# Row gathers tied one by one to ScalarE steps instead of issued in rows, in a kernel of attention and eight routed experts

## The chip, the cores and the metric

The kernel runs on one core of one Trainium2 chip. Its engines are TensorE (PE: matrix products), ScalarE (ACT), VectorE (DVE), GpSimd (POOL: here it issues the indirect DMAs) and SyncE (SP: here it issues plain DMAs). Each takes its instructions in the order of the program and waits on semaphores that the others raise. The metric is device time in microseconds (us), less is better.

## The reference, cut to what matters

```python
qn = q / (norm(q, axis=1) + 1e-6); kn = k / (norm(k, axis=1) + 1e-6)     # 4 batches, 5056 x 256, f32
a = softmax(kn.T @ qn / tau);  x = (v @ a).reshape(20224, 256)
logits = x @ w_gate                                      # 8 experts, each takes 20224/8 = 2528 tokens
# tokens and experts are paired greedily by descending logit until every expert is full
for e in range(8):
    out[mask_e] = maximum(x[mask_e] @ w1[e], 0) @ w2[e]  # 256 -> 1024 -> 256
```

## The kernel before

The attention writes the rows of x to DRAM (`x_d`) in the first 305 us. After it the program goes through eight expert slots, p = 0 to 7; `route` finds out for slot p which expert it is and which tokens it has, in a stream of small DVE, ACT and PE instructions that a planner (`o`) strews between the expert work of the slot before. The order on each engine is fixed when the program is built.

A slot's 2528 tokens are cut into chunks of up to 512 rows (c = 0 to 4; slot 0 has six, the first and the last of them 256). A chunk goes through four steps. `load_x` puts its row gathers into the list `queue`, one for each 128 rows: an indirect DMA by POOL (L1483) from `x_d` into a tile `xg`, with a small memset of `spacer` (L1482) before it; behind the last gather of a chunk SP sends it out and back in blocks (L1468, L1473: tiles `xr`, `xq`). `turn` transposes it on DVE (L1528). `layer1` makes 8 units of 6 matmuls into a PSUM tile `ph`; ACT takes each unit's relu as `hH` (L1680), DVE the rest as `hL` (L1686). `layer2` makes a tile `py` of 24 matmuls for each 128 rows; ACT copies it to `y` (L1731) and POOL scatters it to `out` by an indirect DMA (L1734).

In slots 4 to 7 two chunks are taken together where `MIXED` says so: c = 3 with 4 in each, c = 1 with 2 in slots 6 and 7 too. Such a pair (`layers`) makes the first layer of both by 28 products of three matmuls (L1764) in the order of `STEPS`. Between the products ACT copies one PSUM tile onto another (`cAB`: `ph<-py`, `cBZ`: `ph<-ph`) or into the tile `p7` (L1770) and takes relus (`hi..`, L1790); DVE adds (`j..`, L1774) and makes the low parts (`lo..`, L1793). The next product into a tile waits for the copy.

A gather leaves `queue` at the calls of `gather()`: behind every second unit of `layer1` (every one in most of slot 0), behind each tile of `layer2`, all that are left in `turn_parts` and at the start of `layers`, and behind each product of a pair. None of these waits for the work at whose place it stands: it waits for its tile and its DMA semaphore only, so POOL may run them as soon as it is free. POOL also runs an `IOTA` (tile `G`) once for each route.

Of the kernel before, what the change touches and what calls it, by code (L numbers as in the profile page):

```python
# [14 lines left out]
AF = mybir.ActivationFunctionType  # L15
# [6 lines left out]
E, F = 8, 1024  # L22
# [72 lines left out]
PARTED = (4, 5, 6, 7)  # L95
MIXED = {4: (3,), 5: (3,), 6: (1, 3), 7: (1, 3)}
LOAD_AT = (1, 0)
STEPS = (
# [9 lines left out]
def attention_moe(ctx: ExitStack, tc: tile.TileContext, q, k, vt, tau, wg, w1t, w2t, tabs, out):  # L108
    nc = tc.nc
    V = nc.vector  # L110
    S = nc.scalar
    P = nc.gpsimd
# [7 lines left out]
    x_d = dram.tile([B * NCH * CH, C], F32, name="x_d")  # L120
# [485 lines left out]
    done = {}  # L606
# [719 lines left out]
    o = Order()  # L1326
# [26 lines left out]
    def n_in(col):  # L1353
        return 128 if col < NCOL - 1 else LASTC
# [99 lines left out]
    def load_x(p, c, paced=False):  # L1454
        idx = routed[p]["src"]
        if not chunks_seen:
            chunks_seen.append(ffx.tile([128, PAD_X], F32, name="pad_x", bufs=1))
        xg = ffx.tile([128, 4, C], F32, name="xg", bufs=2)
        xgs[p, c] = xg
        cols = cols_of(p, c)  # L1460
        by_v = (p, c) not in BY_PE
        xr = dram.tile([8, 128, 128], F32, name=f"xr{p}_{c}") if by_v else None

        def blocks():
            back = chunks.index((p, c)) - 2
            o.flush(turn_unit.get(chunks[back], 0))
            n = 2 * len(cols)
            nc.sync.dma_start(xr[0:n].rearrange("i p w -> p i w"), xg.rearrange("p i (k w) -> p (i k) w", k=2)[:, 0:n])  # L1468
            xq = ffx.tile([128, 4, 2, 4, 32], F32, name="xq", bufs=2)
            xgs[p, c] = xq  # L1470
            parts = xr[0:n].rearrange("i (g a) (j m) -> a (i g) j m", a=32, j=4)
            for j in range(4):
                nc.sync.dma_start(xq.rearrange("p i k g m -> p (i k g) m")[32 * j:32 * j + 32, 0:4 * n], parts[:, :, j])  # L1473

        def fetch(i, col, n):
            at = idx[:n, col:col + 1]
            if paced:
                at = ffx.tile([128, 1], I32, name="pace", bufs=4)[:n]
                S.activation(at, idx[:n, col:col + 1], AF.Copy)
            if by_v and n < 128:  # L1480
                P.memset(xg[n:128, i], 0.0)
            P.memset(spacer, 0.0)  # L1482
            P.indirect_dma_start(out=xg[:n, i, :], out_offset=None, in_=x_d,  # L1483
                                 in_offset=bass.IndirectOffsetOnAxis(ap=at, axis=0))
            if i == len(cols) - 1:
                if by_v:
                    blocks()
                landed[p, c] = o.pe + (MOVED_LAT if by_v else GATHER_LAT)
        for i, col in enumerate(cols):
            queue.append((p, c, lambda i=i, col=col, n=n_in(col): fetch(i, col, n)))  # L1490

    def gather():
        for _ in range(2 if queue and queue[0][1] == 0 else 1):
            if queue:
                queue.pop(0)[2]()

    queue = []
    landed = {}
# [22 lines left out]
    def turn_parts(p, c, xg, xH, xL, nt):  # L1521
        raw = ffx.tile([128, 2, 512], F32, name="xg", bufs=2)
        full = nt // 128

        def rotate(kb):
            rows = xg.rearrange("p i k g a -> p k i g a")[:, kb]
            turned_ = raw[:, kb].rearrange("p (i g n) -> p i g n", i=4, g=4)
            V.transpose(turned_[:, 0:full], rows[:, 0:full])  # L1528
            if nt % 128:
                V.transpose(turned_[:, full, 0:nt % 128 // 32], rows[:, full, 0:nt % 128 // 32])  # L1530
                V.memset(raw[:, kb, nt:512], 0.0)

        def mixed(dst, a, b, op):
            turned[0] = later_on(o.pe, 640, lambda: V.tensor_tensor(dst, a, b, op=op))

        def high(dst, src):
            def copy():
                S.activation(dst, src, AF.Copy)
                o.scalar(o.dve, 620)
            later_on(0, 0, copy)  # L1540

        def low(dst, src, h_):
            mixed(dst, src, h_.bitcast(F32), OP.subtract)
        for kb in range(2):
            turn_unit[p, c] = later_on(o.pe, 700, lambda kb=kb: rotate(kb))
        r1, r2 = raw[:, 0], raw[:, 1]
        high(xH[:, 1], r2)
        if c % 2:
            high(xH[:, 0], r1)
            low(xL[:, 1], r2, xH[:, 1])  # L1550
            low(xL[:, 0], r1, xH[:, 0])
            own["raw"] = r1, r2
            return
        a1, a2 = own["raw"]
        sH, sL = s_tiles()
        own["s"] = sH, sL
        low(xL[:, 1], r2, xH[:, 1])
        mixed(r2, r1, r2, OP.add)
        high(sH[:, 0], r2)
        mixed(r1, a1, r1, OP.subtract)  # L1560
        high(xH[:, 0], r1)
        mixed(a1, r2, a1, OP.subtract)
        high(sH[:, 1], a1)
        mixed(a2, a2, a1, OP.subtract)
        high(sH[:, 2], a2)
        low(xL[:, 0], r1, xH[:, 0])
        low(sL[:, 0], r2, sH[:, 0])
        low(sL[:, 1], a1, sH[:, 1])
        low(sL[:, 2], a2, sH[:, 2])
        while queue:  # L1570
            gather()
        at = chunks.index((p, c))
        for p_, c_ in chunks[at + 1:at + 3]:
            want(("idx", p_), lambda p_=p_, c_=c_: load_x(p_, c_))
# [84 lines left out]
    def layer1(p, c, inserts, every=1):  # L1659
# [9 lines left out]
        for fb in range(8):  # L1669
# [4 lines left out]
            for l, x_ in ((wH, xH), (wL, xH), (wH, xL)):  # L1674
                for kb in range(2):
# [1 line left out]
                    PE.matmul(ph[:, 0:nt], lhsT=l[:, w], rhs=x_[:, kb, 0:nt], start=(i == 0), stop=(i == 5))  # L1677
                    i += 1
                    o.tick(nt / 2.4 + 3)
            S.activation(hH[:, fb, 0:nt], ph[:, 0:nt], AF.Relu)  # L1680
            o.scalar(o.pe + 200, 600)

            lows[p, c] = unit[0]
# [3 lines left out]
                                       op0=OP.max, op1=OP.subtract)  # L1687
            o.post(o.pe + LAYER_LAT, 90 + nt, low, phs[-1])
            settle()
            if fb % every == (0 if p == 0 else every - 1):  # L1690
                gather()
        o.inner = False
        return hH, hL

# [13 lines left out]
    def layer2(p, c, h, inserts, behind=()):  # L1708
# [5 lines left out]
        for i, col in enumerate(cols_of(p, c)):  # L1714
# [23 lines left out]
            scat.append(sd)  # L1738
            settle()
            if not any(c + 1 in (f, f + 1) for f in MIXED.get(p, ())):  # L1740
                gather()

    def layers(p, c):
        o.flush(turned[0])
# [4 lines left out]
             "22": (bH[:, 1], bL[:, 1])}  # L1749
        for i, name in enumerate(("s1", "s2", "s4")):  # L1750
            x[name] = sH[:, i], sL[:, i]
        while queue:
            gather()
        h = [[ffx.tile([128, 8, 512], F32R, name=name) for name in ("hH", "hL")] for _ in range(2)]
        seeded = [(ph_tile(), len(phs) - 1) for _ in range(4)]
        fresh = [ps_2.tile([128, 512], F32, name="py") for _ in range(2)]
# [3 lines left out]
        def product(dst, a, b, g, first=False):  # L1760
            n = 0
            f = slice(g * 128, (g + 1) * 128)
            for i, l in ((0, 0), (0, 1), (1, 0)):
# [2 lines left out]
                n += 1  # L1766
                o.tick(227)

        def copy(dst, src):
            S.activation(dst, src, AF.Copy)  # L1770
            o.scalar(o.pe, 600)

        def joined(key, dst, src):
# [1 line left out]
            sums[key] = dst  # L1775
            o.dve += 690

        o.held = True
        for step in STEPS:
            op, g = step.split(".")  # L1780
            g = int(g)
            A, D = fresh[g % 2], fresh[1 - g % 2]
            Bk, Z = seeded[g % 2][0], seeded[2 + g % 2][0]
            if op[0] in "hl":
# [2 lines left out]
                t, f, src = place[op[2:]]  # L1787
                hH, hL = h[t]
                if op[0] == "h":
                    S.activation(hH[:, f], src, AF.Relu)  # L1790
                    o.scalar(o.pe, 600)
                else:
                    V.scalar_tensor_tensor(hL[:, f], src, 0.0, hH[:, f].bitcast(F32), op0=OP.max, op1=OP.subtract)  # L1793
                    o.dve += 690
# [12 lines left out]
            else:  # L1807
# [2 lines left out]
                 "P5": lambda: product(Z, "s1", "t1", g), "P4": lambda: product(Bk, "22", "t4", g),  # L1810
                 "P3": lambda: product(Z, "s4", "22", g)}[op]()
                settle()
                gather()
        o.held = False
        o.dve = max(o.dve, o.pe + PAIR_LAT)
        unit[0] += 1
# [219 lines left out]
```

## Time and profile before

| | us |
|---|---|
| time of the kernel, median of 3 runs (lowest, highest) | 1292.16 (1287.87, 1292.93) |
| the profiled execution's own time | 1292.82 |
| its span in the trace | 1291.0 |
| PE busy in it | 1241.5 (96%) |
| DVE, ACT, POOL busy | 945.2, 644.8, 404.6 |
| mean granted clock of TensorE, share of full | 0.993 |

The span is that of the instructions; the 1.8 us between it and the time lie around it. PE's idle time is the difference of span and busy time. Times in rows count from the span's start.

### The profile page before, as it was taken

Reading aid. Unit: us, or ns where it says so; the run is one execution under the profiler, and the core shown is the slowest. Engines: PE = TensorE matmul, PEld = TensorE weight load, DVE = VectorE, ACT = ScalarE, POOL = GpSimd, SP = SyncE. Lnnn points to the kernel's source line nnn. Section 1 sums busy time; section 2 is a strip of 40 time slices with the busy share of each in tenths; the row PEclk is TensorE's granted clock in tenths of the full one; section 3 lists DMA queues with packets and bytes.
Section 4 is the critical chain, followed back from the end, with each engine's and each line's share of the span. In section 5 each row is a group of like instructions: output and inputs, shape, how many; then the busy total and the mean of one; then the engine's idle time right before and its main releaser. Section 6 shows DMA issues by size and latency. Waiting matters only on the chain.

```text
span 1291.0 us, 23586 instructions
## 1 busy us (share of the span) xinstructions
PE 1241.5 (96%) x8710; PEld 1100.8 (85%) x8710; DVE 945.2 (73%) x2396; ACT 644.8 (50%) x1491; POOL 404.6 (31%) x700
## 2 busy tenths in 40 slices
PE   9999999999899999998999999999999999999998
PEld 7888877998788978887989879889889787978798
DVE  6687597888669678767777978787687776665652
ACT  6556652565324344433433745556564655554552
POOL 0000001001523445343444332634335444233422
PEclk9999999999999999999999999999999999999999
DMA  8999884344222154154432642442563443353500
GB/s 318 313 403 400 302 289 154 144 175 175 87 57 83 54 118 137 39 119 98 139 91 73 141 110 72 131 109 64 104 143 109 103 127 104 74 111 106 113 34 32
DMA packets 222515, 179.37 MB, mean 139 GB/s; under 512 B 152384, under 2 KB 193216, under 8 KB 217792
## 3 DMA queue, kind: packets, MB, share of 16 engines
q1 hardware_dynamic: 195328, 98.41, 28.1%
q0 software_dynamic: 17664, 58.22, 13.9%
q10 hardware_dynamic: 9408, 21.24, 4.2%
q8 instruction: 68, 1.11, 0.4%
q14 instruction: 47, 0.39, 0.1%
HBM read 118.06 MB, written 59.77 MB: 138 GB/s over the span
## 4 chain that ended last, share of the span: by engine, by line
PE 67%; issue 14%; POOL 8%; DMA 5%; DVE 3%; ACT 2%; another core or an unknown queue 0%; POOLq 0%; SPq 0%; ACTq 0%; DVEq 0%
PE py L1726 23%; PE ph L1677 22%; PE s L341 8%; PE px L289 8%; POOL out_dram L1734 4%; POOL xg L1483 3%; DMA x_d<-xs 2%; PE pc L853 2%; DMA ua<-in_q_dram 1%; PE px L467 1%; PE ph L1764 1%; DMA uc<-in_k_dram 1%; PE py L1764 1%; DVE hL L1686 1%; PE pi L1067 1%
## 5 line engine op out<-in xcount | busy, mean ns | idle before, releaser
L1726 PE MATMUL py<-uc,hH 128*128 128x256 f32 (+1 forms) x2560 | 339.4, 280 | 3.2 <-issue 3.2
L1726 PEld LDWEIGHTS py<-uc,hH 128*128 128x128 f32 (+1 forms) x2560 | 314.8, 187 | 7.0 <-issue 5.0
L1677 PE MATMUL ph<-xH,ua 128*128 128x512 f32 (+3 forms) x928 | 254.7, 392 | 3.7 <-issue 2.2
L1734 POOL DMA_INDIRECT out_dram<-y,idx x105 | 109.5, 1043 | 373.9 <-ACT y L1731 349.0
L1680 ACT ACTIVATE hH<-ph 128x512 fp32r<-128x512 f32 (+3 forms) x232 | 133.3, 579 | 157.3 <-PE ph L1677 138.3
L1677 PEld LDWEIGHTS ph<-xH,ua 128*128 128x128 f32 x928 | 168.2, 190 | 36.4 <-issue 4.2
L1686 DVE SCALAR_TENSOR_TENSOR hL<-ph,hH 128x512 fp32r<-128x512 f32 (+3 forms) x232 | 153.3, 663 | 52.2 <-ACT hH L1680 39.0
L1726 PE MATMUL py<-uc,hL 128*128 128x256 f32 (+1 forms) x1280 | 181.1, 279 | 1.7 <-issue 1.7
L1483 POOL DMA_INDIRECT xg<-x_d,src x156 | 155.0, 993 | 60.5 <-issue 56.5
L1726 PEld LDWEIGHTS py<-uc,hL 128*128 128x128 f32 (+1 forms) x1280 | 161.4, 187 | 2.2 <-issue 2.1
L1677 PE MATMUL ph<-xL,ua 128*128 128x512 f32 (+3 forms) x464 | 143.2, 388 | 0.0
L1731 ACT ACTIVATE y<-py 128x256 f32<-128x256 f32 (+1 forms) x105 | 40.2, 383 | 163.0 <-PE py L1726 129.0
L1677 PEld LDWEIGHTS ph<-xL,ua 128*128 128x128 f32 x464 | 86.4, 190 | 17.6 <-issue 1.2
L341 PE MATMUL s<-ua 128*128 128x256 f32 x320 | 74.0, 388 | 3.3 <-DMA ua<-in_q_dram 2.0
L341 PEld LDWEIGHTS s<-ua 128*128 128x128 f32 x320 | 60.9, 193 | 15.5 <-issue 6.0
L292 ACT ACTIVATE xs<-px 128x512 f32<-128x512 f32 (+2 forms) x98 | 49.6, 519 | 47.4 <-PE px L289 45.5
L341 PE MATMUL s<-uc 128*128 128x256 f32 x320 | 71.4, 380 | 0.3 <-DMA uc<-in_q_dram 0.3
L341 PEld LDWEIGHTS s<-uc 128*128 128x128 f32 x320 | 60.3, 190 | 9.4 <-issue 1.5
L289 PE MATMUL px<-aH,vh 128*128 128x256 f32 (+1 forms) x232 | 67.7, 294 | 0.5 <-ACT aH L257 0.5
L289 PE MATMUL px<-aH,vl 128*128 128x256 f32 (+1 forms) x232 | 65.8, 284 | 1.4 <-DVE vl L268 1.4
L1734 POOL DMA_INDIRECT out_dram<-c,idx x33 | 34.0, 1030 | 104.2 <-ACT c L1731 101.6
L289 PE MATMUL px<-aL,vh 128*128 128x256 f32 (+1 forms) x232 | 65.7, 284 | 0.0
(431 smaller groups left out, 2178.4 us busy)
## 6 DMA issues: line engine op xcount, KB each, us to landing
x_d<-xs ACTq DMA_DIRECT2D x39, 512.0 KB
xr<-xg SPq DMA_DIRECT2D x34, 512.0 KB
xq<-xr SPq DMA_DIRECT2D x136, 128.0 KB
vr<-in_vt_dram SPq DMA_DIRECT2D x14, 1024.0 KB
uc<-in_k_dram SPq DMA_DIRECT2D x18, 512.0 KB
uc<-in_q_dram SPq DMA_DIRECT2D x18, 512.0 KB
ua<-in_k_dram SPq DMA_DIRECT2D x17, 512.0 KB
ua<-in_q_dram SPq DMA_DIRECT2D x17, 512.0 KB
```

The costliest lines, as they stand in the source:

```text
L289: mm = PE.matmul(px[:, i * C:i * C + width], lhsT=l_, rhs=a_, start=(j == 0), stop=(j == len(terms) - 1))
L292: S.activation(xs[:, t % TH:t % TH + n, 0:width], px[:, 0:n * width].rearrange("p (t c) -> p t c", t=n), AF.Copy)
L341: newest[0] = PE.matmul(sb[:, ib * C:(ib + 1) * C], lhsT=kt[:, t, ib * 128:(ib + 1) * 128], rhs=qt[:, t, :], start=(first and t == 0 and i ...
L853: PE.matmul(D, lhsT=ge[:, g], rhs=oh[:, 0:Q, cs_], start=(g == 0), stop=(g == COLS // CG - 1))
L1483: P.indirect_dma_start(out=xg[:n, i, :], out_offset=None, in_=x_d, in_offset=bass.IndirectOffsetOnAxis(ap=at, axis=0))
L1677: PE.matmul(ph[:, 0:nt], lhsT=l[:, w], rhs=x_[:, kb, 0:nt], start=(i == 0), stop=(i == 5))
L1680: S.activation(hH[:, fb, 0:nt], ph[:, 0:nt], AF.Relu)
L1686: V.scalar_tensor_tensor(hL[:, fb, 0:nt], ph[:, 0:nt], 0.0, hH[:, fb, 0:nt].bitcast(F32), op0=OP.max, op1=OP.subtract)
L1726: PE.matmul(py[:n, 0:C], lhsT=l[:, fb, tk], rhs=w[:, d], start=(j == 0), stop=(j == 23))
L1731: S.activation(y[:n], py[:n, 0:C], AF.Copy)
L1734: sd = P.indirect_dma_start(out=out, out_offset=bass.IndirectOffsetOnAxis(ap=idx[:n, col:col + 1], axis=0), in_=y[:n], in_offset=None)
L1764: PE.matmul(dst, lhsT=w[b][l][:, f], rhs=x[a][i], start=(first and n == 0), stop=(n == 2), skip_group_check=True)
```

## The change

Each gather of a slot other than 0 now waits, by a semaphore, for one ScalarE instruction: `gather(after)` hands it to `fetch`. In `layer1` one gather stands behind the relu of every unit but the first (slot 0 has its places of before, with the wait). In a pair one stands behind the last ACT step at each of 8 (c = 1) or 10 (c = 3) entries of `GATHER_AT`. In `layer2` none is left between the tiles, except in a slot's last chunk where the next chunk to be gathered is at most two ahead (`rush`); slot 0 keeps its own. The loops that emptied `queue` in `turn_parts` and `layers` are gone. Besides, `o.held`, which keeps the planner's streams out of a pair, is now set in a pair c = 3 only if the next slot's tokens are known by then.

```diff
+GATHER_AT = {1: ("p7.0", "cAB.1", "cBZ.1", "hi12.0", "cAB.2", "p7.2", "hi11.2", "cAB.3"),
+             3: ("p7.0", "cAB.1", "cBZ.1", "hi12.0", "hi21.1", "hi11.2", "cBZ.3", "hi11.3",
+                 "hi12.3", "hi21.3")}
...
-        def fetch(i, col, n):
+        def fetch(i, col, n, after=None):
...
-            P.indirect_dma_start(out=xg[:n, i, :], out_offset=None, in_=x_d,
+            got = P.indirect_dma_start(out=xg[:n, i, :], out_offset=None, in_=x_d,
                                  in_offset=bass.IndirectOffsetOnAxis(ap=at, axis=0))
+            if after is not None:
+                tc.add_manual_dep(got.ins, after.ins.name, SPACED, reason="room between gathers")
...
-    def gather():
-        for _ in range(2 if queue and queue[0][1] == 0 else 1):
-            if queue:
-                queue.pop(0)[2]()
+    def gather(after=None):
+        if queue:
+            queue.pop(0)[2](after)
... turn_parts, and the same in layers:
-        while queue:
-            gather()
... layer1:
-            S.activation(hH[:, fb, 0:nt], ph[:, 0:nt], AF.Relu)
+            relu = S.activation(hH[:, fb, 0:nt], ph[:, 0:nt], AF.Relu)
-            if fb % every == (0 if p == 0 else every - 1):
-                gather()
+            if fb % every == 0 if p == 0 else fb > 0:
+                gather(relu)
... layer2:
             if not any(c + 1 in (f, f + 1) for f in MIXED.get(p, ())):
-                gather()
+                rush = p and c == len(cuts[p]) - 1 and queue and chunks.index(queue[0][:2]) <= chunks.index((p, c)) + 2
+                for _ in range(int(bool(rush)) if p else 2 if queue and queue[0][1] == 0 else 1):
+                    gather()
... layers (last_act[0] is set by each copy and each hi step):
-        o.held = True
         for step in STEPS:
+            o.held = c < 3 or p == E - 1 or bool(done.get(("idx", p + 1)))
...
                 settle()
-                gather()
+            if step in GATHER_AT[c]:
+                gather(last_act[0])
```

On POOL, at the start of the pair c = 3 of slot 6, behind the last scatter of the chunk before, the rows before are

```order
L1734 DMA out_dram<-y,idx 20224x256 [waits DMASW6_49,Activation_49]
L1482 MEMSET spacer 1x1 [waits Pool_49]
L1483 DMA xg<-x_d,src 128x256 [waits DMAHW6_49,DMASW7_49,DVE_49]
L1482 MEMSET spacer 1x1 [waits Pool_49]
L1483 DMA xg<-x_d,src 128x256 [waits DMASW0_49]
L1482 MEMSET spacer 1x1 [waits Pool_49]
L1483 DMA xg<-x_d,src 128x256 [waits DMASW1_49]
```

and those of the changed kernel, in which the lines have moved by three or four, are

```order
L1738 DMA out_dram<-y,idx 20224x256 [waits DMASW6_49,Activation_49]
L1485 MEMSET spacer 1x1 [waits Pool_49]
L1486 DMA xg<-x_d,src 128x256 [waits DMASW7_49,DMAHW6_49,DVE_49,Activation_49]
L1485 MEMSET spacer 1x1 [waits Pool_49]
L1486 DMA xg<-x_d,src 128x256 [waits DMASW0_49,Activation_49]
L1485 MEMSET spacer 1x1 [waits Pool_49]
L1486 DMA xg<-x_d,src 128x256 [waits DMASW1_49,Activation_49]
```

POOL's order is the same here; what moved is the time at which each gather may start, by the added wait for ACT.

On POOL, in a slot without pairs, between two tiles of `layer2` of one chunk and `layer1` of the next, the rows before are

```order
L1734 DMA out_dram<-y,idx 20224x256 [waits DMASW1_49,Activation_49]
L1733 MEMSET spacer 1x1 [waits Pool_49]
L1734 DMA out_dram<-p_9618,idx 20224x256 [waits DMASW2_49,Activation_49]
L1482 MEMSET spacer 1x1 [waits Pool_49]
L1483 DMA xg<-x_d,src 128x256 [waits DMAHW6_49,DMASW3_49,DVE_49]
L1482 MEMSET spacer 1x1 [waits Pool_49]
L1483 DMA xg<-x_d,src 128x256 [waits DMASW4_49]
L1733 MEMSET spacer 1x1 [waits Pool_49]
L1734 DMA out_dram<-y,idx 20224x256 [waits DMASW5_49,Activation_49]
```

and those of the changed kernel are

```order
L1738 DMA out_dram<-p_9594,idx 20224x256 [waits DMASW2_49,Activation_49]
L1737 MEMSET spacer 1x1 [waits Pool_49]
L1738 DMA out_dram<-y,idx 20224x256 [waits DMASW3_49,Activation_49]
L1737 MEMSET spacer 1x1 [waits Pool_49]
L1738 DMA out_dram<-y,idx 20224x256 [waits DMASW4_49,Activation_49]
L1485 MEMSET spacer 1x1 [waits Pool_49]
L1486 DMA xg<-x_d,src 128x256 [waits DMASW5_49,DMAHW6_49,DVE_49,Activation_49]
L1485 MEMSET spacer 1x1 [waits Pool_49]
L1486 DMA xg<-x_d,src 128x256 [waits DMASW6_49,Activation_49]
```

The gathers have moved from between the scatters (L1738) to behind them, each behind a relu.

On ACT, at the start of the pair of slot 5, the rows before, in which `junk` and `ext` belong to the route of slot 6, are

```order
L1129 ACTIVATE junk,sgn<-pi,rhalf 128x160 [waits Activation_49] x2
L1131 ACTIVATE ext<-pi 128x6
L1731 ACTIVATE y<-py 128x256 [waits DMASW4_49,PE_49]
L1770 ACTIVATE ph<-py 128x512 [waits PE_49]
L1770 ACTIVATE p_13033<-py 128x512 [waits DMASW1_49,PE_49]
```

and those of the changed kernel are

```order
L1735 ACTIVATE y<-py 128x256 [waits DMASW4_49,PE_49]
L1132 ACTIVATE junk,sgn<-pi,rhalf 128x160 [waits Activation_49]
L1776 ACTIVATE ph<-py 128x512 [waits PE_49]
L1132 ACTIVATE junk,sgn<-pi,rhalf 128x160 [waits Activation_49]
L1134 ACTIVATE ext<-pi 128x6
L1776 ACTIVATE p_12966<-py 128x512 [waits DMASW1_49,PE_49]
```

Two `junk` and the `ext`, ahead of the last copy to `y` before, stand behind it now, two of the three between the pair's first two copies; the 16 small DVE instructions that follow on them in the route stand inside the pair too.

## Rows read from the trace of the kernel before

**Rows 1.** The page, parts 1 and 2: the span, PE's busy time

```profile
span 1291.0 us, 23586 instructions
...
PE 1241.5 (96%) x8710; PEld 1100.8 (85%) x8710; DVE 945.2 (73%) x2396; ACT 644.8 (50%) x1491; POOL 404.6 (31%) x700
```

**Rows 2.** Engines' busy us by stretch, clock, DMA, GB/s: five layer bursts

```profile
333.20:353.00 19.80, 16.05 (x107) 12.07 (x106) 12.73 (x31) 6.47 (x11) 13.56 (x24) 1.00 0.33 96
...
sum 74.10, PE 61.32 PEld 48.60 DVE 43.48 ACT 27.45 POOL 52.46; mean PE 12.26 PEld 9.72 DVE 8.70 ACT 5.49 POOL 10.49
```

**Rows 3.** The same view: the bursts at the starts of five pairs

```profile
1128.60:1142.00 13.40, 10.83 (x47) 8.02 (x45) 6.03 (x9) 7.51 (x14) 9.31 (x18) 1.00 0.52 140
...
sum 66.10, PE 53.52 PEld 39.94 DVE 32.55 ACT 37.19 POOL 46.26; mean PE 10.70 PEld 7.99 DVE 6.51 ACT 7.44 POOL 9.25
```

**Rows 4.** The same view: six more bursts

```profile
437.50:456.00 18.50, 16.61 (x172) 16.06 (x170) 10.90 (x33) 4.55 (x10) 13.15 (x24) 1.00 0.28 87
822.20:839.20 17.00, 14.97 (x72) 11.53 (x70) 11.78 (x34) 8.72 (x20) 12.11 (x19) 1.00 0.65 153
...
707.20:718.80 11.60, 11.60 (x58) 9.11 (x57) 11.27 (x27) 8.30 (x25) 8.99 (x15) 1.00 0.52 149
...
sum 80.10, PE 72.25 PEld 62.84 DVE 55.96 ACT 35.38 POOL 58.98; mean PE 12.04 PEld 10.47 DVE 9.33 ACT 5.90 POOL 9.83
```

**Rows 5.** PE alone by stretch: all between these bursts

```profile
353.00:437.50 84.50, 83.59 (x717) 0.98 0.22 62
...
768.80:822.20 53.40, 53.40 (x371) 0.97 0.36 95
...
910.20:945.50 35.30, 35.30 (x245) 0.96 0.44 105
...
1142.00:1162.90 20.90, 20.90 (x133) 0.92 0.45 82
...
sum 685.10, PE 681.17; mean PE 48.65
```

**Rows 6.** PE alone by stretch: the first 7.3 us of each pair burst

```profile
1128.60:1135.90 7.30, 7.30 (x33) 1.00 0.30 90
...
sum 36.50, PE 36.50; mean PE 7.30
```

**Rows 7.** POOL's timeline, pair of slot 6: start, us, instruction [idle before, releaser]

```profile
1128.60 0.97 POOL L1734 DMA_INDIRECT out_dram<-y,idx  x1 [1.66 <-ACT y L1731]
...
1129.87 0.98 POOL L1483 DMA_INDIRECT xg<-x_d,src  x1 [0.22 <-issue]
...
1138.66 0.94 POOL L1483 DMA_INDIRECT xg<-x_d,src  x1 [0.23 <-issue]
```

**Rows 8.** ACT's timeline in the same burst

```profile
1141.33 0.58 ACT L1770 ACTIVATE ph<-py 128x512 f32<-128x512 f32 x1 [2.86 <-remote]
```

**Rows 9.** PE's timeline in the same burst

```profile
1141.96 1.18 PE L1764 MATMUL ph<-sH,ub 128*128 128x512 f32 x2 [2.45 <-ACT ph L1770]
```

**Rows 10.** PE's waits over the span: total us, times, longest

```profile
PE ph L1764 <- ACT ph L1770: 9.3, 5, 2.5
```

**Rows 11.** ACT's timeline in the last pair, the one without gathers

```profile
1255.30 0.58 ACT L1770 ACTIVATE ph<-py 128x512 f32<-128x512 f32 x1
```

**Rows 12.** ACT's timeline in a layer1 of slot 3

```profile
708.67 0.60 ACT L1680 ACTIVATE hH<-ph 128x512 fp32r<-128x512 f32 x1
...
710.05 0.60 ACT L1680 ACTIVATE hH<-ph 128x512 fp32r<-128x512 f32 x1 [0.41 <-issue]
```

**Rows 13.** DVE's timeline at the start of slot 5's pair

```profile
1010.98 2.80 DVE L1166 TENSOR_SCALAR at<-sgn 128x12 int32<-128x12 f32 x1 [1.19 <-ACT junk L1129]
...
1016.29 0.69 DVE L1793 SCALAR_TENSOR_TENSOR hL<-py,hH 128x512 fp32r<-128x512 f32 x1 [0.24 <-issue]
```

**Rows 14.** SP's queue in the pair c = 1 of slot 6

```profile
1102.68 2.65 SPq L1473 DMA_DIRECT2D xq<-xr  x4
```

**Rows 15.** DVE's timeline in the same pair

```profile
1112.55 0.57 DVE L1528 STREAM_TRANSPOSE xg<-xq 128x384 f32<-128x384 f32 x1
```

More of the change, by code (lines that the diff above doesn't have):

```diff
@@ L1482, in fetch @@
             P.memset(spacer, 0.0)
-            P.indirect_dma_start(out=xg[:n, i, :], out_offset=None, in_=x_d,
-                                 in_offset=bass.IndirectOffsetOnAxis(ap=at, axis=0))
+            got = P.indirect_dma_start(out=xg[:n, i, :], out_offset=None, in_=x_d,
+                                       in_offset=bass.IndirectOffsetOnAxis(ap=at, axis=0))
+            if after is not None:
+                tc.add_manual_dep(got.ins, after.ins.name, SPACED, reason="room between gathers")
             if i == len(cols) - 1:
@@ L1489, in load_x @@
         for i, col in enumerate(cols):
-            queue.append((p, c, lambda i=i, col=col, n=n_in(col): fetch(i, col, n)))
-    def gather():
-        for _ in range(2 if queue and queue[0][1] == 0 else 1):
-            if queue:
-                queue.pop(0)[2]()
+            queue.append((p, c, lambda after, i=i, col=col, n=n_in(col): fetch(i, col, n, after)))
+    SPACED = mybir.DependencyInfo(mybir.DependencyClass.Sync, mybir.DependencyReason.DATA)
+    def gather(after=None):
+        if queue:
+            queue.pop(0)[2](after)
     queue = []
@@ L1751, in layers @@
             x[name] = sH[:, i], sL[:, i]
-        while queue:
-            gather()
         h = [[ffx.tile([128, 8, 512], F32R, name=name) for name in ("hH", "hL")] for _ in range(2)]
@@ L1767, in product @@
                 o.tick(227)
+        last_act = [None]
         def copy(dst, src):
-            S.activation(dst, src, AF.Copy)
+            last_act[0] = S.activation(dst, src, AF.Copy)
             o.scalar(o.pe, 600)
@@ L1789, in layers @@
                 if op[0] == "h":
-                    S.activation(hH[:, f], src, AF.Relu)
+                    last_act[0] = S.activation(hH[:, f], src, AF.Relu)
                     o.scalar(o.pe, 600)
@@ L1812, in layers @@
                 settle()
-                gather()
+            if step in GATHER_AT[c]:
+                gather(last_act[0])
         o.held = False
```

## The prediction

> **What bounds the kernel now.** I read the page first: TensorE (PE) is busy for 1241.5 of 1291.0 us [rows 1]. PE sets the end, so the question is only in what stretches the other 49.5 us of idle time and the losses of its clock lie. I listed PE's gaps over half a microsecond, saw that most stand where GpSimd (POOL) issues many indirect DMAs in a row, and cut the time from 333 to 1265 us by that: the view of windows shows five bursts of gathers in `layer1` and `layer2` with 61.32 us of PE in 74.10, so 12.78 idle [rows 2], five at the starts of pairs with 53.52 in 66.10, so 12.58 idle [rows 3], six others with 72.25 in 80.10, so 7.85 idle [rows 4]; in all that lies between, PE is busy for 681.17 of 685.10 us, 3.93 idle [rows 5]. So 33.2 of 37.1 idle us stand in 220 us of bursts.
>
> One burst shows what the bursts do. After a scatter at 1128.60 eight gathers follow, from 1129.87 to 1138.66, one every (1138.66 - 1129.87) / 7 = 1.256 us [rows 7]. Near its end PE stands still for 2.45 us for a copy `ph<-py` of ScalarE (ACT), which itself stood idle for 2.86 us, released by something that the profile can't name ("remote"), until 1141.33 [rows 8, 9]. The copy's input was long written. In the pair without gathers the same copy runs with no wait [rows 11]. Now (1141.33 - 1128.60) / 9 = 1.414 us: if each of the nine DMAs takes 1.41 us of something behind POOL through which the hand-overs between engines pass too, while POOL issues one each 1.256, the lag grows by 0.16 us a DMA, and what is handed over late in a burst comes late. It fits that PE is never idle in the first 7.3 us of the five pair bursts, in which the scatter and some five gathers go out (36.50 busy of 36.50 [rows 6]), so that all 12.58 idle us stand in what is left of them; 9.3 of these are waits for that copy, up to 2.5 each [rows 10]. I call it the backlog. It is inferred, not seen. The other 3.3 us are waits for other steps of ACT and DVE in the same late parts.
>
> A burst also costs clock. Right behind some of them the granted clock is at its lower level for a while, 1.2 of 2.4 GHz, which shows as means below 1.00: 84.5 us at 0.98 lose 1.7 us, 53.4 at 0.97 lose 1.6, 35.3 at 0.96 lose 1.4, 20.9 at 0.92 lose 1.7 [rows 5]. The bursts ahead of them hold the idle time above; in the stretches themselves PE is busy nearly throughout, so that this is work at half speed, on top of the idle time.
>
> **The change, part by part.**
>
> *Gathers of the pairs.* The rows of the order say that they keep their places on POOL and get a wait for ACT; 8 stand behind ACT steps that lie over some 12 to 15 us of the pair, one per 1.5 us or more in the mean, where POOL issued one per 1.256. Behind POOL stands nothing that the pair needs: only later gathers, and the scatters of the next tiles. At 1.41 us a DMA the lag is then at most that of two or three neighbouring steps. I take the whole 12.6 us as gained [rows 3]. Bounds: nothing, if the waits have another cause, and 12.6.
>
> *Gathers of the layers.* They leave the places between `layer2`'s scatters and stand one behind each relu. Two relus stand 1.38 us apart [rows 12], as long as a DMA takes by the backlog, so that four gathers of a chunk in four units build no lag of their own. But scatters that are late from the tiles before, and an expert's end with its `rush`, still put three to five DMAs behind one another; by the new order I count about a third of the old length in such places. So two thirds of 12.78 are gained, 8.5 us; bounds 4.3 and 12.8 [rows 2]. Of the other bursts, that of slot 4's start (822 us, 17.00 - 14.97 = 2.03 idle) is shortened, half is taken, 1.0; the rest keep their order [rows 4].
>
> *Clock.* The lower level behind the two pair bursts goes (1.4 + 1.7 = 3.1 us); of the two behind layer bursts (1.7 + 1.6) two thirds, 2.2. Together 5.3 [rows 5].
>
> *The route inside slot 5's pair.* By the new `o.held` its tail (two `junk`, the `ext`, some 16 small DVE instructions) moves inside. There it meets the `IOTA` of POOL, which the new order puts there too. Before, that same piece took DVE from 1010.98 to the pair's first operation at 1016.29, 5.31 us, of which 2.80 in one instruction on 12 elements a partition, beside which the `IOTA` ran [rows 13]. ACT's part is short, but DVE's stands ahead of the pair's `j` and `lo` steps, for which PE waits. Bounds: nothing (the pair's DVE has idle time) and 4.8 us (all but half a microsecond). I take the middle, 2.4, lost.
>
> *Late data.* In a pair c = 1 the last gather goes out some 3.3 us later, and the pair is some 2.5 us shorter. SP sent the last blocks from 1102.68, done at 1105.33; their transpose ran at 1112.55 [rows 14, 15], 7.2 us after. That leaves 7.2 - 5.8 = 1.4 us for the transfer itself. It may be late by about one microsecond in each of two pairs: bounds 0 and 2, taken as nothing, since DVE is far less busy than PE there (32.55 against 53.52 [rows 3]).
>
> *Added waits themselves.* A semaphore more on POOL's DMA costs PE nothing as such; the ACT steps have no new instruction.
>
> Sum: 12.6 + 8.5 + 1.0 + 5.3 - 2.4 = 25.0 us. The profiled execution took 1292.82, so 1267.8, rounded to **1268**. That execution is 0.66 above the median, less than the three runs differ (1287.87 to 1292.93); I don't correct for it. About 0.5%, 6.5 us, can be told from no change here.
>
> **The rivals.**
>
> *The gain stands in the pairs only (18%).* In the layers the 1.38 us between relus is a shade below 1.41, and the scatters come on top: the backlog may stay as it is, only later. For it: in the burst at 437 us gathers alternate with scatters and PE still loses 1.89 us [rows 4]. Against it: in the burst at 707 us seven gathers, a scatter and a weight load leave PE without any idle time [rows 4], so a little room is enough. Time: 1292.8 - 12.6 - 3.1 + 2.4 = 1279.5.
>
> *The waits have another cause (10%).* The bursts stand at the starts of pairs and ends of chunks, where PE depends on ACT and DVE anyway, and where the route's chains run. A rule by which DMAs could not hold up engines would say so. Then nothing but the route's move is felt: 1292.8 to 1295. Against it stands above all the pair without gathers, in which the copy `ph<-py` doesn't wait [rows 11], and the "remote" release [rows 8]. The Trainium skill has such a rule ("SBUF — State Buffer", section Who interferes with whom): DMA never contends with a compute engine for that memory's ports, and only VectorE and GpSimd share a pair. By that rule the sum would hold nothing of the bursts. The trace doesn't agree as far as waits go: 33.2 of 37.1 idle us lie in bursts; the rule speaks of ports only, not of hand-overs.
>
> *Slower: the gather delays the ACT step's hand-over (5%).* Each gather now starts just as the ACT step ends on which PE's next product waits. If POOL's issue (0.97 us [rows 7]) holds up that hand-over each time, rather than only when a lag has grown, the 40 gathers of five pairs cost 40 x 0.97 = 38.8 us, and the time is 1267.8 + 38.8 = 1306.6. It is slower than before from 25.0 / 40 = 0.63 us each. Against it: before, the first five gathers of each pair burst go out beside copies and relus without any idle time of PE [rows 6].
>
> *As forecast: 67%.* That case's own range: with all of the layers (12.8), the whole of 822's 2.0, the whole clock (6.4) and a free route the gain is 33.8, so 1259; with a third of the layers (4.3) and of their clock (1.1), nothing at 822, a route of 4.8 and late data of 2.0 it is 12.6 + 4.3 + 4.2 - 4.8 - 2.0 = 14.3, so 1278.5.
>
> **How the numbers follow.** Faster by over 0.5%: forecast and first rival, 0.67 + 0.18 = 0.85. Within 0.5%: 0.10. Slower: 0.05. The range of 1258 to 1286 holds the forecast's own range and the first rival with its dear route (1279.5 + 2.4, and 4 us for a part of the pairs' gain that fails); it leaves out the second and the third, 0.15, and little else.
>
> **What would show it.** In the changed kernel's trace: POOL's gathers in pairs 1.3 us or more apart in nearly all places; no `ph<-py` of ACT released by "remote"; PE's wait for ACT's `ph` in pairs near nothing, from 9.3 us; the stretches behind the first and fourth pair at a clock of 1.00; layer bursts with about 4 us of idle PE in all. In slot 5's pair one wait of PE of 2 us or so for DVE. The prediction is wrong if PE still waits at the same steps though the gathers are apart (the second rival), if many short waits of PE follow the ACT steps named in the table (the third), or if the idle time of the layers only moves to later units (the first).

## The result and the profile after

The changed kernel takes 1257.92 us (median of 4 runs, 1255.64 to 1259.74) against 1292.12 of before in the same place: 0.9731 of it, 95% interval [0.9708, 0.9755], 34.2 us less. The prediction was 1268 with a range that began at 1258. The profiled execution took 1259.74, 33.1 us less than that of before, and the parts below are told against these two.

One thing has to be known for all that follows. The runs of this study were made in jobs, each with runs of the kernel before beside it, and the kernel before took 1290 to 1297 us in some of them (that of the result too) and 1240 us in others. Ratios are formed within one job.

The page of the changed kernel, to be read beside [rows 1]:

```profile
span 1258.0 us, 23692 instructions
...
PE 1230.8 (98%) x8710; PEld 1099.2 (87%) x8710; DVE 944.8 (75%) x2396; ACT 646.0 (51%) x1491; POOL 400.0 (32%) x700
```

PE is idle for 1258.0 - 1230.8 = 27.2 us, 22.3 less than before, and busy for 10.7 less. To place both I cut the new trace at the same matmuls at which the windows of before begin and end. The five pair bursts, beside [rows 3]:

```profile
993.55:1005.11 11.56, 9.97 (x44) 7.88 (x44) 10.71 (x31) 7.31 (x14) 5.34 (x10) 1.00 0.13 35
...
1102.09:1112.45 10.36, 10.36 (x47) 8.28 (x46) 5.94 (x9) 7.94 (x14) 5.25 (x10) 1.00 0.22 63
...
sum 52.93, PE 51.34 PEld 41.23 DVE 35.32 ACT 38.77 POOL 27.06; mean PE 10.27 PEld 8.24 DVE 7.06 ACT 7.75 POOL 5.41
```

66.10 us have become 52.93, so 13.2 are gone; the idle time left, 52.93 - 51.34 = 1.59 us, all stands in slot 5's pair. PE's busy time fell too, from 53.52 to 51.34, with the same 231 matmuls. The five layer bursts, beside [rows 2]:

```profile
334.55:351.17 16.62, 15.42 (x107) 12.07 (x106) 12.56 (x31) 6.47 (x11) 11.18 (x21) 1.00 0.27 80
...
sum 62.57, PE 59.40 PEld 48.93 DVE 44.17 ACT 29.54 POOL 37.36; mean PE 11.88 PEld 9.79 DVE 8.83 ACT 5.91 POOL 7.47
```

74.10 have become 62.57, 11.5 gone, 3.17 idle left. (In one of the five, from 574.23 us, the route's small matmuls lie elsewhere, so that 63 stand in it in place of 49; those of the layer are the same to one.) Of the others [rows 4] I show slot 4's start (17.00 before), slot 5's end (11.50 before) and slot 6's end (12.90 before):

```profile
807.79:821.78 13.99, 13.99 (x70) 11.81 (x69) 12.21 (x26) 9.50 (x26) 8.42 (x16) 1.00 0.24 74
1022.98:1032.21 9.23, 9.23 (x83) 8.93 (x83) 8.16 (x17) 3.72 (x13) 7.83 (x12) 1.00 0.73 213
1131.77:1145.17 13.40, 10.43 (x86) 10.09 (x86) 5.91 (x10) 3.69 (x9) 9.49 (x17) 0.93 0.53 172
...
sum 75.09, PE 70.44 PEld 62.92 DVE 55.92 ACT 37.28 POOL 51.20; mean PE 11.74 PEld 10.49 DVE 9.32 ACT 6.21 POOL 8.53
```

The first has lost all its idle time, 3.0 us of length, and the second 2.3 us; in the third gathers still stand in a row behind scatters, and it has not gained. The stretches behind bursts, PE alone, beside the four of [rows 5]; the last one is the stretch behind slot 6's end, 25.90 us long before:

```profile
351.17:434.12 82.95, 82.03 (x717) 1.00 0.24 70
755.92:807.79 51.87, 51.87 (x372) 1.00 0.41 107
890.54:924.55 34.01, 34.01 (x247) 1.00 0.55 139
1112.45:1131.77 19.32, 19.32 (x134) 1.00 0.76 151
1145.17:1171.89 26.72, 26.72 (x160) 0.91 0.24 55
```

Four of them are at the full clock now and shorter by 1.55, 1.53, 1.29 and 1.58 us, 5.95 in all; the last is 0.82 longer. In the pair of slot 6, the one shown before, POOL's gathers now start like this:

```profile
1103.78 0.99 POOL L1486 DMA_INDIRECT xg<-x_d,src  x1 [0.64 <-ACT p L1776]
...
1105.99 0.96 POOL L1486 DMA_INDIRECT xg<-x_d,src  x1 [1.13 <-ACT ph L1776]
...
1112.76 0.94 POOL L1486 DMA_INDIRECT xg<-x_d,src  x1 [1.63 <-ACT hH L1796]
```

They are 2.2 and 2.3 us apart (1112.76 is the fifth), each released by ACT, where they were 1.25. The copy `ph<-py` that stood idle for 2.86 us before [rows 8] has no wait:

```profile
1111.26 0.58 ACT L1776 ACTIVATE ph<-py 128x512 f32<-128x512 f32 x1
```

### The profile page after: what moved, and what is told of

Read it like the earlier page. It is cut to its first block, busy times and chain, and to the rows that moved or that the text cites. A ratio compares the mean times of both kernels' runs of the same rounds, so it can differ in the third digit from the quotient of the medians.

```text
span 1258.0 us, 23692 instructions
## 1 busy us (share of the span) xinstructions
PE 1230.8 (98%) x8710; PEld 1099.2 (87%) x8710; DVE 944.8 (75%) x2396; ACT 646.0 (51%) x1491; POOL 400.0 (32%) x700
## 3 DMA queue, kind: packets, MB, share of 16 engines
q1 hardware_dynamic: 195328, 98.41, 28.1%
## 4 chain that ended last, share of the span: by engine, by line
PE 69%; issue 11%; POOL 6%; DMA 6%; DVE 5%; ACT 2%; POOLq 0%; SPq 0%; ACTq 0%; DVEq 0%
PE py L1730 23%; PE ph L1681 23%; PE px L292 8%; PE s L344 8%; POOL out_dram L1738 3%; POOL xg L1486 3%; DMA x_d<-xs 2%; PE pc L856 2%; PE ph L1768 2%; DMA ua<-in_q_dram 1%; PE px L470 1%; PE py L1768 1%; DMA uc<-in_k_dram 1%; PE pi L1070 1%; DMA uc<-in_q_dram 1%
## 5 line engine op out<-in xcount | busy, mean ns | idle before, releaser
L1681 PE MATMUL ph<-xH,ua 128*128 128x512 f32 (+3 forms) x928 | 251.5, 388 | 1.0 <-DVE xL L1618 0.9
L1738 POOL DMA_INDIRECT out_dram<-y,idx x105 | 108.0, 1029 | 290.1 <-ACT y L1735 264.9
L1738 POOL DMA_INDIRECT out_dram<-c,idx x33 | 33.1, 1002 | 81.8 <-ACT c L1735 80.7
```

The costliest lines, as they stand in the source:

```text
L1738: sd = P.indirect_dma_start(out=out, out_offset=bass.IndirectOffsetOnAxis(ap=idx[:n, col:col + 1], axis=0), in_=y[:n], in_offset=None)
```

## Experiments

Runs of one job shared a chip and the runs of the kernel before.

| job | run | us | before | ratio, 95% |
|---|---|---|---|---|
| 1 | e1 pairs only | 1239.95 | 1239.93 | 1.000 [0.999, 1.001] |
| 1 | e2 layers only, streams held | 1266.58 | | 1.0218 [1.020, 1.024] |
| 1 | e3 new order, no wait | 1244.20 | | 1.0038 [1.003, 1.005] |
| 1 | e4 before, three memsets | 1242.11 | | 1.0021 [1.001, 1.003] |
| 2 | e5 the change again | 1262.08 | 1296.41 | 0.9755 [0.972, 0.979] |
| 2 | e6 before, no memset | 1293.66 | | 0.9967 [0.994, 1.000] |
| 2 | e7 the change, streams held | 1279.09 | | 0.9884 [0.985, 0.992] |
| 3 | e8 as e1 | 1239.80 | 1239.75 | 0.9998 [0.999, 1.001] |
| 3 | e9 layers only | 1244.78 | | 1.0041 [1.003, 1.006] |
| 3 | e10, e11 as e3, e4 | 1245.41, 1242.03 | | 1.0046, 1.0015 |
| 4 | e12, e13 as e4, e3 | 1242.19, 1245.41 | 1240.41 | 1.0013, 1.0047 |
| 4 | e14 mix | 1242.14 | | 1.0017 [1.001, 1.003] |
| 5 | e15 the change again | 1245.79 | 1239.77 | 1.0046 [1.003, 1.006] |
| 5 | e16 as e4 | 1241.76 | | 1.0021 [1.001, 1.003] |
| 6 | e17 as e4 | 1246.75 | 1296.81 | 0.9625 [0.958, 0.967] |
| 7 | e18 as e3 | 1291.05 | 1290.74 | 1.0005 [0.998, 1.003] |

e8, e10 to e13 and e16 repeat e1, e3 and e4 with the same theories; they met the 1240 us condition again, in which they can't tell the theories apart.

**The halves.** e1 (and e8) leaves out the edits of `layer1`, `layer2` and `o.held`; e2 leaves out those of the pairs and `o.held`; e9 is e2 with the new rule for `o.held`.

```diff
 e1, against the changed kernel
-            if fb % every == 0 if p == 0 else fb > 0:
-                gather(relu)
+            if fb % every == (0 if p == 0 else every - 1):
+                for _ in range(2 if queue and queue[0][1] == 0 else 1):
+                    gather()
 ... and in the same way `rush` and the loop in layer2
 e2 and e9, in layers (and the loops that empty the queue, in turn_parts and at the start of layers, are back)
-            if step in GATHER_AT[c]:
-                gather(last_act[0])
+                gather()
 e1 and e2
-            o.held = c < 3 or p == E - 1 or bool(done.get(("idx", p + 1)))
+            o.held = True
```

> Of the change only the gathers in the pairs are kept: one behind each listed ACT step, with the wait; the gathers of the layers are where they were before, without a wait, and no route runs inside a pair. Backlog theory (each indirect DMA takes 1.41 us of something behind POOL, and hand-overs between engines are late by the lag): the five pair bursts lose 13 to 15 us and the clock behind two of them 3.4, so 1292.1 - 17 = 1275 (1273 to 1278), and the layer bursts keep their 12 to 13 us of idle PE. Rival, another cause (the waits at pair starts come from ACT and DVE themselves): 1290 to 1294, the copies wait as before.

> The other half alone: the gathers of the layers behind relus and out of the second layer, the gathers of the pairs emptied at their start and behind products as before, without a wait; no route inside a pair. Backlog: the layer bursts lose 11.5 us, the one at slot 4's start 3.0, the clock behind two of them 3.2, so 1292.1 - 17.7 = 1274 (1272 to 1278); the pair bursts keep 12 us of idle PE. If the gain of both halves is not additive (each half only hides the other's lag), the sum of the two gains differs from 34.2 us by more than 5. Rival, only the pairs gain: 1289 to 1293.

> The layers' half alone, this time with the new rule for the held streams (without it slot 6's first rows are late by 13 us): gathers of the layers behind relus, those of the pairs in bursts at the pair's start and behind products, without a wait. Backlog: the layer bursts' 11.5, slot 4's start 3.0, clock 3.2, less the route in the pair 2: 15 to 17 us below before, 0.988 of it, and the two halves add up to the whole (34 us) within 5. If the halves overlap: their sum is over 40 or under 28. In a job in which before takes 1240: 3 to 6 above it.

e1 took what the kernel before took, which here was 1239.93 us: nothing to gain. e9 shows why. Its pairs have the bursts of before, and POOL's rows in that of slot 6 read

```profile
1093.33 0.97 POOL L1740 DMA_INDIRECT out_dram<-y,idx  x1 [1.67 <-ACT y L1737]
...
1094.61 0.99 POOL L1486 DMA_INDIRECT xg<-x_d,src  x1 [0.21 <-issue]
...
1103.42 0.95 POOL L1486 DMA_INDIRECT xg<-x_d,src  x1 [0.22 <-issue]
```

(1103.42 - 1094.61) / 7 = 1.259 us from gather to gather, as before [rows 7]. But ACT's copy, at the step where it was late for 2.86 us, has no wait in ACT's timeline:

```profile
1102.51 0.58 ACT L1780 ACTIVATE ph<-py 128x512 f32<-128x512 f32 x1
```

and in the view of windows PE is never idle in that burst:

```profile
1094.30:1105.50 11.20, 11.20 (x51) 9.22 (x51) 7.23 (x11) 8.70 (x16) 8.40 (x18) 1.00 0.50 145
```

So the same row of DMAs at the same pace does not hold up anything in the 1240 us condition. The two halves were not met in the other one, so whether they add up there was not tried. e2 missed for another reason, which e7 tells.

**The streams in the pair.** e7 is the changed kernel with `o.held = True` in pairs, as in e2.

> The changed kernel with the planner's streams kept out of every pair, as before. The second run (layers alone) showed PE idle for 13.2 us at 1032 us, for the data of slot 6's first chunk, and half the clock for 17 us behind it. If that comes of the late gathers together with the route that ends behind the pair, it comes here too: 20 us (16 to 25) above the changed kernel on the same chip, and the edit of the held streams is what makes the moved gathers possible. If it came of the emptied queues of that run alone: 1.5 to 4 us below the changed kernel, the price of the route inside slot 5's pair.

It took 17.0 us more than the change in its job, as the first of the two cases said. PE's row behind the end of slot 5:

```profile
1052.49 2.24 PE L1681 MATMUL ph<-xH,ua 128*128 128x512 f32 x4 [13.41 <-ACT xH L1613]
```

13.41 us of waiting for slot 6's first rows, after which the clock was at 1.2 GHz for a time (0.50 of full from 1052 to 1056 us). With the streams held out, slot 6's route ends behind the pair, and its gathers, which no longer go out at the first opportunity, follow later still. The edit of `o.held` is what lets the gathers of the layers be moved; those of the pairs alone (e1) do without it. In e9 (with it) the wait is gone, while e2 (without it) has 13.2 us of the same wait.

**The memsets.** e6 takes away the memset ahead of each gather, e4 (and e11, e12, e16, e17) sets three, in the kernel before; nothing is moved and no wait for ACT added.

```diff
+            for _ in range(3):
-            P.memset(spacer, 0.0)
+                P.memset(spacer, 0.0)
```

> The kernel before without the small memset ahead of each gather: POOL issues a gather each 1.0 us or so in a burst, in place of 1.25. Backlog: on a chip that takes 1.41 us for each the lag grows by 0.4 us a DMA in place of 0.16 and the ten bursts lose 2 to 3 us more each, 1310 to 1325. On a chip without waits at 1.25 us it tells the bound: if it takes under 1.0 us, 1238 to 1242 with no idle time in bursts; if it takes 1.1 to 1.25, waits of 0.5 to 2.5 us late in each burst, 1248 to 1270. Rival, another cause than the rate: within 3 us of the kernel before on the same chip.

POOL's rows of e6 show that its premise was wrong: without the memset a gather still follows each 1.25 to 1.29 us. The run tells nothing on the rate, only that one memset costs nothing.

```profile
901.26 0.99 POOL L1482 DMA_INDIRECT xg<-x_d,src  x1 [0.31 <-issue]
902.55 0.97 POOL L1482 DMA_INDIRECT xg<-x_d,src  x1 [0.30 <-issue]
```

> The kernel before, in which three small memsets stand before each gather in place of one: nothing is moved and no wait for ACT is added, only POOL issues a gather each 1.85 us in place of 1.25. Backlog: 1.85 is over 1.41, so that the lag doesn't grow; most of the waits in bursts go: 1258 to 1266, the copies in pairs without a remote wait. Rival, the tie to ACT or the place makes the gain: 1290 to 1296, with the same waits.

> The kernel before with three memsets ahead of each gather, alone in its job. Where before takes 1290 to 1300 us: 0.973 to 0.98 of it by the backlog of 1.41 us a DMA, since 1.47 us from gather to gather lets no lag grow; 0.995 or above if the tie to ACT or the place in the order makes the gain. Where before takes 1240: 1242 again.

Three memsets did not make the 1.85 us that e4's text expected. e17 is the one run of this edit in the 1290 us condition, and the one that decides. In the pair burst of slot 6 a gather goes out each (1108.18 - 1097.12) / 7 = 1.58 us, five of the seven steps being 1.47 to 1.52, by POOL's timeline:

```profile
1097.12 0.98 POOL L1484 DMA_INDIRECT xg<-x_d,src  x1 [0.67 <-issue]
1098.11 0.38 POOL L1483 MEMSET spacer<- 1x1 f32 x3
1098.64 0.96 POOL L1484 DMA_INDIRECT xg<-x_d,src  x1 [0.15 <-issue]
...
1108.18 0.94 POOL L1484 DMA_INDIRECT xg<-x_d,src  x1
```

The windows of its five pair bursts, cut at the same matmuls as those of before, read

```profile
1095.10:1105.47 10.37, 10.37 (x47) 8.28 (x46) 5.94 (x9) 7.94 (x14) 7.75 (x25) 1.00 0.26 68
...
sum 51.25, PE 51.25 PEld 41.24 DVE 32.56 ACT 39.34 POOL 38.28; mean PE 10.25 PEld 8.25 DVE 6.51 ACT 7.87 POOL 7.66
```

the sum of those of its five layer bursts

```profile
sum 61.28, PE 59.21 PEld 49.10 DVE 43.03 ACT 28.56 POOL 47.49; mean PE 11.84 PEld 9.82 DVE 8.61 ACT 5.71 POOL 9.50
```

and ACT's timeline at the copy that was late

```profile
1104.28 0.58 ACT L1771 ACTIVATE ph<-py 128x512 f32<-128x512 f32 x1
```

66.10 us have become 51.25 with no idle time, 74.10 have become 61.28, and the copy has no wait. 0.9625 of before is better than was expected (0.973 to 0.98), and better than the change in its two jobs (0.9731 and 0.9755). Room between the gathers is enough, with no new place and no wait for ACT. Whether it is their rate that counts or the number of transfers under way at once, this edit can't tell.

**The wait.** e3 (and e10, e13, e18) keeps the new order and `o.held`, and leaves the added wait out:

```diff
-            if after is not None:
-                tc.add_manual_dep(got.ins, after.ins.name, SPACED, reason="room between gathers")
```

> The changed kernel with its order, but without the added waits for ACT: the gathers may run as soon as POOL reaches them. Backlog: in the pairs POOL issues one each 1.25 us again, PE waits 2.5 us or so for the copy in each, and the clock falls behind two: 1257.9 + 13 + 3.4 = 1274; in the layers the order alone keeps the scatters free, and a part of the bursts comes back: 1274 to 1284 in all. Rival, the place in the order makes the gain, not the room in time: 1257 to 1260.

> The changed kernel's order without the added waits, alone in its job. Where before takes 1290 to 1300 us: the pair bursts come back, since POOL issues one gather each 1.25 us there (13 us of PE and 3.4 of clock), while in the layers four gathers in a row behind scatters that are 2.7 us apart build little lag: 0.983 to 0.988 of before. If the wait adds nothing and the place makes the change's gain: 0.973 to 0.976 as the change itself. If the wait makes all of it: 0.997 to 1.003. Where before takes 1240: 1244 to 1246 again.

e18 missed: it took as much as the kernel before, where I had expected the layers' part of the gain. The windows of its pair bursts, cut at the same matmuls, read

```profile
1126.95:1140.37 13.42, 10.82 (x47) 8.02 (x45) 6.04 (x9) 7.52 (x14) 9.41 (x18) 1.00 0.53 140
...
sum 63.15, PE 53.03 PEld 40.09 DVE 35.61 ACT 36.59 POOL 46.69; mean PE 10.61 PEld 8.02 DVE 7.12 ACT 7.32 POOL 9.34
```

those of its layer bursts

```profile
578.49:599.76 21.27, 14.54 (x64) 10.69 (x63) 9.66 (x18) 6.82 (x14) 11.52 (x19) 0.69 0.84 163
...
sum 77.49, PE 64.17 PEld 51.88 DVE 44.66 ACT 28.16 POOL 49.55; mean PE 12.83 PEld 10.38 DVE 8.93 ACT 5.63 POOL 9.91
```

and the view of PE's waits (total us, times, longest)

```profile
PE ph L1766 <- ACT ph L1774: 8.1, 5, 2.4
PE ph L1679 <- DVE xL L1616: 6.7, 2, 4.0
```

ACT's timeline at the copy has the late release of before [rows 8] again:

```profile
1139.70 0.58 ACT L1774 ACTIVATE ph<-py 128x512 f32<-128x512 f32 x1 [2.85 <-remote]
```

The pairs lose 63.15 - 53.03 = 10.1 us again, and PE's waits for the copy are back, 8.1 us against 9.3 before [rows 10]. In the layers 74.10 us have become 77.49: without the wait the gathers collect behind the last scatter, not four in a row but eight. In the stretch from 578 us these nine DMAs start 1.26 us apart, 21.27 - 14.54 = 6.7 us are idle, and the mean clock is 0.69. The idle time is the second row of waits: PE waits for low parts `xL`, these for ACT's `xH`, and that stands behind a relu which ACT started at 585.97, after 2.27 us without work, released by "remote". The rows themselves were there: their transpose ran at 584.34. In e3, the same program in the 1240 us condition, this wait is 0.9 us. The new place without room in time gains nothing.

**The change in either condition, and a mix.** e5 and e15 are the changed kernel itself. e14 has the waits of the pairs, and the layers of before with three memsets.

> The changed kernel unaltered, beside the kernel before on the same chip. The kernel before took 1292.1 us where the change was timed and 1239.9 where the four runs so far were made, in the latter with no idle time of PE in any burst. If the gain hangs on a condition of the chip (how fast what lies behind POOL takes an indirect DMA: 1.41 us there, less than 1.25 here), the change has nothing to gain on a chip like the second: before 1240, changed 1243 to 1248, slower by the route in slot 5's pair (1.6 us of wait in the same order without the added waits); on a chip like the first: 1258 against 1292. If the gain is the kernel's own, 0.973 of before on either.

> The changed kernel unaltered, again beside the kernel before. In a job in which before takes 1290 to 1300 us: 0.973 to 0.976 of it, as twice before. In one in which it takes 1240: 1243 to 1246 (1.003 to 1.005 of before), since there the bursts cost nothing, and its new order alone, without the added waits, took 1244.2 to 1245.4; if the added waits have a price of their own, 1247 or more.

> A version of both: in the pairs the gathers behind the listed ACT steps with the wait, in the layers at their places of before with three memsets ahead of each; no route inside a pair, so that slot 5's pair has no 1.6 us of wait and no rows come late. Where before takes 1290 to 1300, by the backlog: 0.970 to 0.978 of before, as the changed kernel or 2 to 4 us better. If only a tie to ACT helps: 0.987 (the pairs' half). Where before takes 1240: 1240 to 1242, below the changed order's 1244.

Where before takes 1240 us, the change is 0.46% slower (e15), as much as its order without the wait (e3, e10, e13: 0.4 to 0.5%); e9, whose pairs have no such wait, lies there too. So most of the loss is that of the order and of the route in slot 5's pair, not of the waits. The mix was met in that condition only: 1242.14, the price of the memsets. Of e15, the page's first lines:

```profile
span 1245.4 us, 23692 instructions
...
PE 1225.1 (98%) x8710; PEld 1096.5 (88%) x8710; DVE 944.7 (76%) x2396; ACT 646.2 (52%) x1491; POOL 401.5 (32%) x700
```

Its span is 1258.0 - 1245.4 = 12.6 us shorter than that of the same program in the result's job.

## Why the prediction was right in kind and short in size

The cause that it named holds where the change was timed: with more room between POOL's DMAs and nothing else changed, the waits go (e17), and with the new places but no room they stay (e18). What of the chip takes the DMAs, and why not in each job, stays open.

The prediction called its backlog inferred, not seen. The trace has it: it keeps increments of semaphores with their times, of which the views print only the releaser ("remote" where none of the instructions that raise the semaphore ended near it). In the burst of slot 6's pair before, the increments that PE's matmuls make stand 0.01 us behind the end of their matmul up to 1135.71 us. PE's last matmul ahead of its stop ends at 1139.52; increments of that semaphore stand at 1139.19, 1141.31 and 1141.38, and the copy starts at 1141.33. In the same burst of e9 and of e17 every one that is kept stands 0.01 us behind its matmul. Over the whole trace, 47 increments of PE come more than 1 us after any matmul that makes one has ended in the kernel before, 31 in e18, 14 in the changed kernel, 8 in e17 and 2 in every trace of the 1240 us condition. Those of ACT and DVE, as far as they are kept, do so at most twice in every trace. So it is PE's hand-over that is seen to come late, not the hand-overs between engines in general. And the lag does not grow by 0.16 us a DMA from the first one, as the prediction had it: behind a scatter and five gathers there is none yet, at the end it is 1.8 us at least, where the working gives 1.4. The 1.41 us a DMA is no measured capacity.

*Gathers of the pairs, with the route.* Forecast 12.6 - 2.4 = 10.2; measured 13.2. The step that failed is that the worth of a burst was read from PE's idle time. A part of each stop counts as busy, which hid 53.52 - 51.34 = 2.2 us. PE's timeline in slot 6's pair before shows how:

```profile
1136.89 0.61 PE L1764 MATMUL py<-xH,ua 128*128 128x512 f32 x2
1137.35 0.39 PE L1764 MATMUL py<-xL,ua 128*128 128x512 f32 x1
1137.86 0.73 PE L1764 MATMUL ph<-sH,ua 128*128 128x512 f32 x2
```

In an unbroken stream a matmul starts (1137.35 - 1136.89) / 2 = 0.23 us after the one before it, but its row counts 0.39. So the next one could have started at 1137.58; it started at 1137.86, 0.28 later, of which only the last 0.12 are idle, and the two behind the stop took 0.73 in place of 0.61. (The 1.18 us of [rows 9] are another matter: that row starts 0.04 us ahead of the window's end, at the start of the stretch with the lower clock [rows 5].) The route costs 1.6 in place of 2.4, by PE's timeline in slot 5's pair of the changed kernel

```profile
998.09 0.74 PE L1768 MATMUL py<-xH,ub 128*128 128x512 f32 x2 [1.59 <-DVE hL L1799]
```

and by DVE's timeline there:

```profile
992.49 2.25 DVE L1169 TENSOR_SCALAR at<-sgn 128x12 int32<-128x12 f32 x1 [3.17 <-ACT junk L1132]
...
997.35 0.68 DVE L1799 SCALAR_TENSOR_TENSOR hL<-py,hH 128x512 fp32r<-128x512 f32 x1
```

As forecast, `at` runs beside the `IOTA` (2.25 us for 12 elements), its chain now stands ahead of the pair's low part, and PE waits for that.

*Gathers of the layers.* Forecast 8.5 (a third kept); measured 11.5: 3.2 of 12.8 idle us are kept, a quarter, and 1.9 more were hidden in busy time (61.32 - 59.40). The bound above, 12.8, took only idle time and was too low as a bound; both together are 14.7.

*Slot 4's start.* Forecast 1.0, half; measured 3.0: its 2.0 idle us went whole, with 1.0 of hidden stall.

*Clock.* Forecast 5.3; measured 5.95 - 0.82 = 5.1, near by luck in part: all of the four stretches' loss came back, where two thirds of the layers' were counted, and a fifth stretch, in none of the terms, took some of it. The level fell where a burst was left, behind slot 6's end, and stayed longer there (0.91 over 26.72 us, from 0.93 over 25.9).

*Late data.* Taken as nothing, right for pairs c = 1. The danger was at another place, slot 6's first rows (e7), where the edit of `o.held`, which I had booked only as a loss, saves 17 us.

The forecast's 25.0 and the trace's 33.1 differ by 8.1: 3.0 in the pairs, 3.0 in the layers, 2.0 at slot 4's start, -0.2 of clock, 2.3 at slot 5's end, which the prediction put at nothing ("the rest keep their order"), and -2.0 in all other stretches, of which 1.35 lie ahead of the first burst (it begins at 334.55 us, from 333.20). So the terms sized by idle time are the ones that failed. The range's lower end rested on the same idle time and was 0.1 us too high: with the hidden 2.2 + 1.9 + 1.0 us and slot 5's 2.3 the best case would have been 33.8 + 7.4 = 41.2 us, 1251.6.

*The rivals.* Gain in the pairs only: out, the layers gave 11.5. (In the burst at 707 us, which was held against it, POOL's rows have six gathers, not seven.) Another cause: out by e17. The gather that delays each hand-over: out; in four of the five pair bursts of the changed kernel PE has no idle time at all, and in the fifth it waits for DVE. And with the wait in place the change took 1245.8 in the 1240 us condition, without it 1244.2 to 1245.4, so that it costs at most 1.6 us, not 38.8. The rule "SBUF — State Buffer", Who interferes with whom, of the Trainium skill speaks of memory ports; what e17 shows is not against it, and it gave no price for this. That the time of before hangs on the job was in none of my cases.

## What to carry to other kernels

When engines wait late in a row of DMAs that one engine issues back to back, space the row first, by idle instructions on the issuing engine: it needs no new order, and here it gave more (0.9625) than the change that tied each DMA to other work (0.973). Where the row held up nothing, in the 1240 us condition, the memsets cost 0.1 to 0.2% and the change 0.5%. The worth of such a stall is the shortening of the whole stretch between two fixed matmuls, since a part of it hides in busy time (4.1 of 24.7 us in the ten bursts). And a change that takes transfers out of the first possible place must be asked at each of them what then comes late; the worst place (13 us) was not where the gathers had moved most.

## What was not expected of the hardware

The kernel before, the very same program, took 1290 to 1297 us in four jobs (medians) and 1240 us in four others; the programs of the change, of e3 and of e4 met both as well. A good part of the difference lies in the bursts. e18 and e3 are one program, with spans of 1287.9 and 1241.9 us. Of the 46.0 us between them 28.1 lie in the ten bursts, which in e18 took 63.15 (pairs) and 77.49 (layers), and in e3, cut at the same matmuls,

```profile
sum 52.97, PE 51.37 PEld 41.25 DVE 35.31 ACT 38.78 POOL 43.11; mean PE 10.27 PEld 8.25 DVE 7.06 ACT 7.76 POOL 8.62
...
sum 59.58, PE 58.65 PEld 49.20 DVE 44.49 ACT 29.30 POOL 45.18; mean PE 11.73 PEld 9.84 DVE 8.90 ACT 5.86 POOL 9.04
```

Of 52 us (1292 against 1240) the change gets back 34, of 57 (1297 against 1240) the memsets 50. Durations are the same in both, for instance POOL's gather (0.94 to 0.99 us) and ACT's copy (0.58). In the one condition 1.26 us from DMA to DMA leaves no wait (e9). In the other, waits are seen with 1.26 (e18) and none with 1.58 (e17's pair).

The traces differ in one more way. The page's part 6 gives the time from issue to landing in every trace of the 1240 us condition and in none of the other. For the same DMA, first in the kernel before, then in e4:

```profile
x_d<-xs ACTq DMA_DIRECT2D x39, 512.0 KB
...
x_d<-xs ACTq DMA_DIRECT2D x39, 512.0 KB, 2.8
```

Records of semaphore increments are missing in the first: the trace of the kernel before has 7860 by DMAs, that of e4, with the same DMAs, 10672. Up to 305 us, ahead of the first gather (313 us), they have as many (2458 and 2464), so that the loss lies where POOL's row DMAs run. e17 lacks them too (8157), with its waits gone. Whatever sets the condition thus reaches the recording of semaphores as well. Every run has its span from such a record, so that the recording itself is the load is not ruled out. What sets the condition the runs don't tell; it is not the chip's number, which was the same in jobs 1 and 2.
